# Float64 weights split on chip: two mantissa-bit steps of VectorE become a ScalarE copy and one shift-and-mask, and eight squares move to VectorE

## The chip, the cores and the metric

The kernel runs on one core of a Trainium2 chip. The metric is the device time of one execution, in microseconds; lower is better. Five engines run at the same time, each in the order of its own program: TensorE (PE, whose weight loads the profile lists as PEld), VectorE (DVE), ScalarE (ACT), GpSimd (POOL) and SyncE (SP, which here only issues transfers). They wait for each other through semaphores.

## The reference

Three layers follow each other: masked attention over 4 batches, 8 heads, 576 positions and 64 columns; a dense layer with a squared ReLU; and a mixture of 8 experts.

```
scores = scale * q @ k.T ; scores = where(mask, scores, -1e9)   # half of the heads local, half strided
attn = softmax(scores) @ v                      # -> x, 2304 tokens x 512
h = x @ w_in ; r = max(h, 0) ; g = s * (r * r) + b ; x = g @ w_out       # w_in, w_out: float64
skip_score = x @ w_skip ; e = argmax(x @ w_gate)
out = x + gate * relu(x @ w1[e]) @ w2[e]        # where skip_score > 0, else out = x
```

`w_in` (512 x 2048) and `w_out` (2048 x 512) come as 64-bit floats and are converted on the chip.

## The kernel before

**Products.** Each 32-bit matrix is kept as an upper part in the form that TensorE reads (F32R) and the rest that the upper part leaves; a product is three matmuls: upper with upper, upper with rest, rest with upper.

**Dense layer.** The 2304 tokens are 6 blocks of 384 and the 2048 hidden columns are 16 chunks. A step `i` is one block with one chunk: `mm1` (12 matmuls into tile `h`), `relu`, the square, `g_hi` and `g_lo` (upper part and rest), then `mm2` (9 matmuls that add into `x2p0` to `x2p2`). Steps 0 to 7 are block 0 with chunks 0 to 7; steps 8 to 23 are block 1 with all chunks; then block 0 goes on. So step 8 is the first that reads block 1's tokens and takes weights that step 0 has used already. After step 7 three copies (`keep`) set block 0's sums aside.

**Attention.** 32 pairs of heads, three units each. The 24 units of batches 0 and 1 come first, around steps 0 to 7. A unit is `scores` (PE, tile `sc`), `top` and `bias` (DVE), `exps` (ACT, one instruction pair per slice), `eps`, `recip`, `norm` (DVE), `turned` (PE, tile `pt`), `moved` (ACT, tile `pts`), `mixed` (PE, tile `xo`), and `put` (ACT and DVE, into `xb`, the dense layer's input). In the second batch `sc`, `pt`, `pts` and `xo` have one buffer each: the next unit's scores wait until the exponentials of the last have read theirs. Block 1's tokens are complete only when the last unit of batch 1 has been put.

**Weights.** The 32 chunks of `w_in` and `w_out` arrive as raw 64-bit words in one of three staging buffers. A word is read as a low and a high 32-bit half (`lw`, `hw`). `scale` (ACT) multiplies the high half by a power of two, which moves the exponent; `shift`, `sign` and `low` (DVE) move it three bits up, and bring in the sign and the three top bits of the low half; `upper` (ACT, or DVE for chunks 0 to 7) and `rest` (DVE) make the two parts.

**Order.** A planner (`Plan.order`) places every task by its estimated cost, its dependencies, its buffers and a priority, on the first engine that is free among those that it may run on. The programs of all engines come out of this one list. So a changed task moves the others on all engines.

Of the kernel before, what the change touches and what calls it, by code (L numbers as in the profile page):

```python
# [8 lines left out]
F32R = mybir.dt.float32r  # L9
BF16 = mybir.dt.bfloat16  # L10
I32 = mybir.dt.int32
AF = mybir.ActivationFunctionType
ALU = mybir.AluOpType
AX = mybir.AxisListType
# [13 lines left out]

PTS_N, HI_N, LO_N, NORM_N = 1, 8, 4, 0

BYPE, SQ_A = 8, 8


FIRST = (-1000.0, 0.0, 26.0, 48.0)
# [119 lines left out]
def kernel(  # L154
# [18 lines left out]
    PE, V, A, G, SY = nc.tensor, nc.vector, nc.scalar, nc.gpsimd, nc.sync  # L173
# [3 lines left out]
    x2d = dp.tile([NT, DM], F32, name="x2d")  # L177
    lst = dp.tile([NE * NT, 2], I32, name="lst")

# [20 lines left out]
    idb = ident.bitcast(BF16)[:, 1::2]  # L200
    toks = wp.tile([128, NTT], I32, name="toks")

# [3 lines left out]
    plan = Plan(CAPS)  # L206
    pools = {"s_": sp, "pts": sp, "r": sp, "sm": sp, "gh": gp, "gl": gp, "row": rp, "lo": rp, "h": ph, "sc": pm, "pt": pm, "xo": pm}

    def make(b, shape, dt):
        tag = b.tag  # L210
        pool = pools.get(tag) or (px if tag.startswith("x2p") else wp)
        return pool.tile(shape, dt, name=tag, bufs=CAPS.get(tag, 1))


    def c_pe(n, k=1, f32=True):
        return {"PE": k * ((4 if f32 else 1) * n / 2400 + 0.008)}

    def c_v(n, fast=1, psum=0.0):
        return {"V": 0.06 + n / fast / 960 + psum}

    def c_a(n, psum=False):
        return {"A": (0.13 if psum else 0.16) + n / 1400}
# [4 lines left out]
    def c_dma(n):  # L227
        return {"SP": max(0.06, n / 360e3)}
# [3 lines left out]
    def copy(e, dst, src):  # L232
        if e == "A":
            A.copy(dst, src)  # L234
        else:
            ENG[e].tensor_copy(dst, src)
# [76 lines left out]
    def add_unit(n, b, hp, g, loc, qk, vt, vbuf, qbuf, nq, nk, by_pe, prio, lq, lv):  # L313
# [40 lines left out]
        def exps(e):  # L354
# [3 lines left out]
            for i in range(nt):  # L358
                A.activation(sv[:, i, :], src[:, i, :], AF.Exp, bias=sm[0:nq, i:i + 1], scale=0.125, accum_out=sm[0:nq, 4 + i:5 + i])

# [87 lines left out]
    def fill(e):  # L448
        d_fill[0] = make(fill_b, [128, 2 * NE * NT // 128], I32)
        G.memset(d_fill[0][:], NOWHERE)  # L450
# [5 lines left out]
    t = plan.add({"G": 0.3}, fill, 6, take=[fill_b])  # L456
# [4 lines left out]

    order = [("i", 0), ("i", 1)]
    for c in range(NFC):
        order.append(("o", c))
# [3 lines left out]
    for n, (m, c) in enumerate(order):  # L470

        z = max(n, len(order) - NSTG + n % NSTG)
        raw_b, c_b = Buf([f"w{order[z][0]}{order[z][1]}"]), Buf(["row", "lo"])
        w_b = wbuf[m, c] = Buf([f"w{m}{c}"])
        wt = win_t if m == "i" else wout_t
        prio = min(PLACE[0, c], PLACE[1, c]) - LEAD + (0.5 if m == "o" else 0.0)
        d = {}

        def stage(e, d=d, raw_b=raw_b, m=m, c=c):
            raw = make(raw_b, [128, 1024], I32)  # L480
            SY.dma_start(raw[:], (w_in if m == "i" else w_out)[:, c].bitcast(I32))
            rv = raw[:].rearrange("p (n t) -> p n t", t=2)
            d["lw"], d["hw"] = rv[:, :, 0], rv[:, :, 1]

        def scale(e, d=d, c_b=c_b):
            c_ = make(c_b, [128, 512], I32)
            d["ci"], d["cv"] = c_[:], c_[:].bitcast(F32)
            A.mul(d["cv"], d["hw"].bitcast(F32), 2.0 ** -112)

        def shift(e, d=d):  # L490
            V.tensor_scalar(d["ci"], d["ci"], 3, 0x7FFFFFF8, op0=ALU.logical_shift_left, op1=ALU.bitwise_and)

        def sign(e, d=d):
            V.scalar_tensor_tensor(d["ci"], d["hw"], -(1 << 31), d["ci"], op0=ALU.bitwise_and, op1=ALU.bitwise_or)  # L494

        def low(e, d=d):
            V.scalar_tensor_tensor(d["ci"], d["lw"], 29, d["ci"], op0=ALU.logical_shift_right, op1=ALU.bitwise_or)

        def upper(e, d=d, w_b=w_b, wt=wt, c=c):
            wt[c] = make(w_b, [128, 2, 512], F32R)  # L500
            copy(e, wt[c][:, 0, :], d["cv"])

        def rest(e, d=d, wt=wt, c=c):
            ENG[e].tensor_tensor(wt[c][:, 1, :], d["cv"], wt[c][:, 0, :].bitcast(F32), op=ALU.subtract)

        t = plan.add(c_dma(128 * 8 * 512), stage, prio - 2, take=[raw_b], lat=DMA)
        t = plan.add(c_a(512), scale, prio, after=[t], take=[c_b], use=[raw_b])
        t = plan.add(c_v(512, 2), shift, prio, after=[t], use=[c_b])
        t = plan.add(c_v(512), sign, prio, after=[t], use=[c_b, raw_b])
        t = plan.add(c_v(512), low, prio, after=[t], use=[c_b, raw_b])  # L510
        t = plan.add({**c_a(512), **(c_v(512, 2) if c < HI_N else {})}, upper, prio, after=[t], take=[w_b], use=[c_b])
        w_done[m, c] = [plan.add(c_v(512), rest, prio, after=[t], use=[c_b])]

# [133 lines left out]
    def route_exp(blk):  # L647
        d = rt[blk]
        d["x8"] = sp.tile([128, 3, 8], F32, name="x8")
        A.activation(d["x8"][:], d["lg"][:, :, 0:8], AF.Exp)  # L650

# [143 lines left out]
    def up(N, f0=0, f1=NFE):  # L795
        for f in range(f0, f1):
# [6 lines left out]
            h = K["h"][f]  # L803
            A.activation(h[:, 0, 0:N], p[:, 0:N], AF.Relu)  # L804
            V.scalar_tensor_tensor(h[:, 1, 0:N], p[:, 0:N], 0.0, h[:, 0, 0:N].bitcast(F32), op0=ALU.max, op1=ALU.subtract)  # L805
# [210 lines left out]
    for i, (blk, fc, begins, ends) in enumerate(SEQ):  # L1016
        h_b, r_b, gh_b, gl_b = Buf(["h"]), Buf(["r"]), Buf(["gh"]), Buf(["gl"])
        d = {}
# [12 lines left out]
        def relu(e, d=d, r_b=r_b):  # L1031
            d["r"] = make(r_b, [128, BLK], F32)
            A.activation(d["r"][:], d["p"][:, 0:BLK], AF.Relu)  # L1033

# [3 lines left out]
        def g_hi(e, d=d, i=i, gh_b=gh_b):  # L1038
            gh = make(gh_b, [128, BLK], F32R)
            A.activation(gh[:], d["r"][:], AF.Identity, bias=sbc[:, 1:2])  # L1040
            gt[i] = [gh]
# [6 lines left out]
        def square_a(e, d=d):  # L1048
            A.activation(d["r"][:], d["r"][:], AF.Square)

# [24 lines left out]
        after = [mm1s[-1] if mm1s else None] + (x_tasks[blk] if fc == 0 else [])  # L1075
        m1 = plan.add(c_pe(BLK, 12, False), mm1, i - 3000, after=after + (w_done["i", fc] if blk < 2 else []), take=[h_b], use=[wbuf["i", fc]])
        mm1s.append(m1)
        t = plan.add(c_a(BLK, True), relu, i - 9000, after=[m1], take=[r_b], use=[h_b])
        if i < SQ_A:
            t = plan.add(c_a(BLK), square_a, i - 9000, after=[t], use=[r_b])  # L1080
            t = plan.add(c_v(BLK, 2), scale_g, i - 9000, after=[t, consts], use=[r_b])
        else:
            t = plan.add(c_v(BLK), square, i - 9000, after=[t, consts], use=[r_b])
        t = plan.add(c_a(BLK), g_hi_a if i < SQ_A else g_hi, i - 9000, after=[t], take=[gh_b], use=[r_b])
        t = plan.add(c_v(BLK), g_lo_a if i < SQ_A else g_lo, i - 9000, after=[t], take=[gl_b], use=[r_b, gh_b])
        gts[i] = t
        if i < NS - 2:
            t = plan.add(c_pe(DM, 9, False), mm2, i + 1.2 - 3000, after=[t, mm2s[-1] if mm2s else None] + (w_done["o", fc] if blk < 2 else []),
                         take=xbuf if begins else [], use=[gh_b, gl_b, wbuf["o", fc]])
# [170 lines left out]
```

## Time and profile before

| | |
|---|---|
| time before, median of 3 runs | 763.52 us (763.04 to 766.59) |
| profiled execution, its own time | 763.24 us |
| its span, first to last instruction | 761.4 us |
| TensorE busy | 734.9 us, 97% of the span |
| VectorE busy | 375.4 us, 49% |
| ScalarE busy | 296.0 us, 39% |

The busy shares are means over the whole span. The work on weights lies in the first 140 us, and what an engine lacks there is read from that stretch.

### The profile page before, as it was taken

The page shows a single profiled execution, that of the slowest core. Times are in us where ns is not written, and L with a number is a line of the kernel's source. Part 1 is how long each engine was busy: PE and PEld are TensorE (multiplying, and loading weights), DVE is VectorE, ACT ScalarE, POOL GpSimd, SP SyncE. Part 2 cuts the span into 40 slices and gives each one's busy share as a digit, 9 for nine tenths or more (in the row PEclk, how much of TensorE's full clock was granted, in tenths as well). Part 3 has the DMA queues.
Part 4 walks back from the last instruction along what each step waited for, and adds up shares of the span by engine and source line. Part 5 has one row for each costly group of instructions (what it writes and reads, how often), then busy time and mean ns, then how long its engine had stood idle before and what let it go on. Part 6 is the DMA issues. An engine that isn't in the chain of part 4 may idle for free.

```text
span 761.4 us, 11904 instructions
## 1 busy us (share of the span) xinstructions
PE 734.9 (97%) x4410; PEld 633.1 (83%) x4411; DVE 375.4 (49%) x1009; ACT 296.0 (39%) x813; POOL 62.7 (8%) x67
## 2 busy tenths in 40 slices
PE   9899989999999999999999999999999999999992
PEld 6788779998888888888888999898787888888791
DVE  4899999624565644456554324654442222313120
ACT  4787766424343543445453223533301402112020
POOL 0000000000010100010001002010032212011121
PEclk9999999999999999999999999999999999999997
DMA  9676685102231222012020005320214502011130
GB/s 294 221 208 207 201 280 142 51 0 84 76 113 48 71 65 80 27 48 78 27 84 1 2 1 174 107 80 5 79 36 142 220 37 75 14 42 56 43 72 32
DMA packets 23505, 69.00 MB, mean 91 GB/s; under 512 B 5035, under 2 KB 5291, under 8 KB 23430
## 3 DMA queue, kind: packets, MB, share of 16 engines
q1 hardware_dynamic: 19350, 56.81, 22.7%
q0 software_dynamic: 3936, 11.03, 4.7%
q8 instruction: 41, 0.67, 0.4%
q14 instruction: 34, 0.28, 0.1%
q10 hardware_dynamic: 144, 0.22, 0.1%
HBM read 52.94 MB, written 15.11 MB: 89 GB/s over the span
## 4 chain that ended last, share of the span: by engine, by line
PE 85%; DMA 5%; DVE 4%; issue 4%; ACT 1%; POOL 0%; POOLq 0%; DVEq 0%; ACTq 0%
PE h L1028 26%; PE x2p L1071 25%; PE h L801 10%; PE x2p L814 9%; DMA out<-row,ids 5%; PE sc L341 3%; PE xo L390 2%; PE pt L373 2%; PE sc L599 1%; PE pt L585 1%; PE h L1180 1%; PE h L341 1%; PE x2p L864 1%; PE h L1024 1%; DVE row L494 0%
## 5 line engine op out<-in xcount | busy, mean ns | idle before, releaser
L1028 PE MATMUL h<-xb,wi 128*128 128x384 f32 x1152 | 225.1, 344 | 2.0 <-ACT wi L234 1.2
L1028 PEld LDWEIGHTS h<-xb,wi 128*128 128x128 f32 x1152 | 203.9, 189 | 8.1 <-ACT wi L234 1.7
L1071 PE MATMUL x2p<-wo,gh 128*128 128x512 f32 x564 | 194.6, 399 | 0.0
L1071 PEld LDWEIGHTS x2p<-wo,gh 128*128 128x128 f32 x564 | 106.1, 188 | 20.1
L1071 PE MATMUL x2p<-wo,gl 128*128 128x512 f32 x282 | 111.1, 394 | 0.6 <-DVE gl L1061 0.4
L801 PE MATMUL h<-xb,wi 128*128 128x512 f32 (+1 forms) x480 | 103.3, 374 | 2.3 <-DVE row L818 1.8
L801 PEld LDWEIGHTS h<-xb,wi 128*128 128x128 f32 x480 | 83.4, 188 | 20.6 <-issue 2.8
L814 PE MATMUL x2p<-wi,wo 128*128 128x512 f32 x432 | 99.4, 390 | 0.0
L1036 DVE SCALAR_TENSOR_TENSOR r<-r,sbc 128x384 f32<-128x384 f32 x88 | 54.3, 617 | 85.7 <-ACT r L1033 85.6
L814 PEld LDWEIGHTS x2p<-wi,wo 128*128 128x128 f32 x432 | 80.8, 188 | 16.6
L1033 ACT ACTIVATE r<-h 128x384 f32<-128x384 f32 x96 | 47.0, 489 | 116.5 <-PE h L1028 111.2
L1040 ACT ACTIVATE gh<-r,sbc 128x384 fp32r<-128x384 f32 x88 | 54.3, 617 | 77.5 <-PE x2p L1071 53.6
L1045 DVE SCALAR_TENSOR_TENSOR gl<-r,sbc,gh 128x384 fp32r<-128x384 f32 x88 | 54.3, 617 | 59.1 <-ACT gh L1040 57.8
L804 ACT ACTIVATE wo<-h 128x512 fp32r<-128x512 f32 (+1 forms) x40 | 22.2, 554 | 144.0 <-PE h L801 139.1
L805 DVE SCALAR_TENSOR_TENSOR wo<-h,wo 128x512 fp32r<-128x512 f32 (+1 forms) x40 | 25.5, 638 | 76.5 <-ACT wo L804 72.3
L1071 PEld LDWEIGHTS x2p<-wo,gl 128*128 128x128 f32 x282 | 53.1, 188 | 9.4 <-DVE gl L1061 0.7
L703 POOL DMA_INDIRECT lst<-pay,ii x18 | 18.4, 1020 | 466.1 <-DVE ii L697 444.9
L818 DVE SCALAR_TENSOR_TENSOR row<-x2p,ids,xb 128x512 f32<-128x512 f32 x14 | 10.5, 751 | 61.8 <-PE x2p L814 61.8
L390 PEld LDWEIGHTS xo<-pts,vl 96*64 96x64 f32 (+1 forms) x480 | 16.9, 135 | 12.5 <-issue 4.5
L390 PE MATMUL xo<-pts,vl 96*64 96x64 f32 (+1 forms) x480 | 21.6, 226 | 3.6 <-DVE xb L397 2.1
L819 POOL DMA_INDIRECT out<-row,ids x14 | 13.9, 995 | 107.5 <-DVE row L818 93.2
L397 DVE TENSOR_TENSOR xb<-xo,xb 128x192 fp32r<-128x192 f32 (+4 forms) x59 | 18.3, 336 | 5.8 <-ACT xb L234 5.6
(479 smaller groups left out, 769.1 us busy)
## 6 DMA issues: line engine op xcount, KB each, us to landing
wo<-in_w SPq DMA_DIRECT2D x16, 512.0 KB, 5.8
qks<-in_qkstr SPq DMA_DIRECT2D x7, 882.0 KB, 6.5
wo<-in_w_out SPq DMA_DIRECT2D x12, 512.0 KB, 3.7
x2d<-row SPq DMA_DIRECT2D x21, 256.0 KB, 3.9
qkl<-in_qkloc SPq DMA_DIRECT2D x6, 864.0 KB
wo<-in_w_in SPq DMA_DIRECT2D x10, 512.0 KB, 4.0
out<-row SPq DMA_DIRECT2D x18, 256.0 KB, 2.0
wi<-in_w_in SPq DMA_DIRECT2D x6, 512.0 KB
```

What stands on the lines that cost most here:

```text
L341: PE.matmul(sc[0:nq, i * nk:(i + 1) * nk], qt, qk[0][:, k0:k0 + nk], start=not by_pe, stop=not by_pe or i == nt - 1)
L390: PE.matmul(xo[64 * h:64 * h + 64, c:c + m], vt[h][:, t, :], d["pts"][0:nk, r:r + m], start=True, stop=True)
L801: PE.matmul(p[:, 0:N], W[f][:, w, k * 128:(k + 1) * 128], x[:, k, 0:N], start=n == 0, stop=n == 11)
L804: A.activation(h[:, 0, 0:N], p[:, 0:N], AF.Relu)
L805: V.scalar_tensor_tensor(h[:, 1, 0:N], p[:, 0:N], 0.0, h[:, 0, 0:N].bitcast(F32), op0=ALU.max, op1=ALU.subtract)
L814: PE.matmul(y[:], K["h"][f][:, g, c], W[NFE + f][:, w, :], start=n == 0, stop=n == 3 * NFE - 1)
L1028: PE.matmul(p[:, 0:BLK], win_t[fc][:, w, k * 128:(k + 1) * 128], x[:, k, :], start=n == 0, stop=n == 11)
L1033: A.activation(d["r"][:], d["p"][:, 0:BLK], AF.Relu)
L1036: V.scalar_tensor_tensor(d["r"][:], d["r"][:], sbc[:, 0:1], d["r"][:], op0=ALU.mult, op1=ALU.mult)
L1040: A.activation(gh[:], d["r"][:], AF.Identity, bias=sbc[:, 1:2])
L1045: V.scalar_tensor_tensor(gl[:], d["r"][:], sbc[:, 1:2], gt[i][0][:].bitcast(F32), op0=ALU.add, op1=ALU.subtract)
L1071: PE.matmul(x2p[t][:], g[:, c], wout_t[fc][:, w, :], start=begins and n == 0, stop=ends and n == 2)
```

## The change

The first four chunks that are converted keep the old steps. For the other 28, after `scale` has read the high half, ScalarE copies the upper 16 bits of the low half over the lower 16 bits of the high half (`beside`); VectorE then shifts the high half right by 13 with its sign kept and masks it, so that the sign and the three bits stand where they belong (`ends`, in place in the staging buffer, every second 32-bit word); and `merge` shifts the scaled value and joins it. Before, three VectorE instructions stood there (`shift`, `sign`, `low`), now two of VectorE and one of ScalarE.

`SQ_A` goes from 8 to 0: steps 0 to 7 no longer square on ScalarE (`square_a`, then `scale_g` on VectorE, a plain copy `g_hi_a` and a subtraction `g_lo_a`), but as the later steps do (`square` on VectorE, `g_hi` with a bias on ScalarE, `g_lo` on VectorE).

```diff
-BYPE, SQ_A = 8, 8
+BYPE, SQ_A = 8, 0
+
+ODD = 4
...
+            hv = raw[:].bitcast(U16).rearrange("p (n t) -> p n t", t=4)
+            d["from"], d["to"] = hv[:, :, 1], hv[:, :, 2]
...
+        def beside(e, d=d):
+            A.copy(d["to"], d["from"])
+
+        def ends(e, d=d):
+            V.tensor_scalar(d["hw"], d["hw"], 13, 7 - (1 << 31), op0=ALU.arith_shift_right, op1=ALU.bitwise_and)
+
+        def merge(e, d=d):
+            V.scalar_tensor_tensor(d["ci"], d["ci"], 3, d["hw"], op0=ALU.logical_shift_left, op1=ALU.bitwise_or)
...
-        t = plan.add(c_v(512, 2), shift, prio, after=[t], use=[c_b])
-        t = plan.add(c_v(512), sign, prio, after=[t], use=[c_b, raw_b])
-        t = plan.add(c_v(512), low, prio, after=[t], use=[c_b, raw_b])
+        if n < ODD:
+            t = plan.add(c_v(512, 2), shift, prio, after=[t], use=[c_b])
+            t = plan.add(c_v(512), sign, prio, after=[t], use=[c_b, raw_b])
+            t = plan.add(c_v(512), low, prio, after=[t], use=[c_b, raw_b])
+        else:
+            t = plan.add(c_a(512), beside, prio, after=[t], use=[raw_b])
+            t = plan.add(c_v(512, 2), ends, prio, after=[t], use=[raw_b])
+            t = plan.add(c_v(512), merge, prio, after=[t], use=[c_b, raw_b])
```

All engines' programs are the same up to step 0 (about 40 us in the trace), and TensorE's program is the same again from step 8 on. Between them it holds the same matmuls in another order. In the rows below, line numbers of the changed kernel are 3 higher in the attention part and 22 higher in the dense part.

ScalarE, between the exponentials of the last unit but one and those of the last unit of batch 1. Before there are four instructions between them: the last copy `g_hi_a` of step 7, a `scale`, an `upper` and the `pts` copy of an earlier unit.

```order
L359 ACTIVATE s__1369,sm<-sc,sm 108x54 x4
L1056 CAST gh<-r 128x384
L488 ACTIVATE row<-wi_1336 128x512
L234 CAST wo_1396<-row 128x512
L234 COPY pts<-pt 54x432
L359 ACTIVATE s__1424,sm<-sc,sm 108x54 x3
```

In the changed kernel there are ten at that place (L508 is `beside`, L237 a copy: into `row` one of the three `keep` copies, into `wo` and `wi` three `upper`, into `xb` two of `put`, into `pts` two `moved`).

```order
L362 ACTIVATE s__1399,sm<-sc,sm 108x54 x4
L508 COPY wo_1352<-wo_1352 128x512
L237 COPY row<-x2p_843 128x512
L237 COPY pts<-pt 54x432
L237 CAST wo_1429<-lo 128x512
L237 CAST wi_1443<-row 128x512
L237 CAST wo_1453<-row 128x512
L237 CAST xb_89<-xo 128x12x6
L237 CAST xb_90<-xo 128x12x12
L237 COPY pts<-pt 54x432
L237 COPY row<-x2p_847 128x512
L362 ACTIVATE s__1470,sm<-sc,sm 108x54 x3
```

Ahead of the first of these rows the changed program has, from the `relu` of step 7 on, eight more: `relu`, the exponentials of the unit before, `scale`, `g_hi`, `beside`, `scale`, `beside`, `scale`. Behind the last row it has, up to the last unit's `pts` copy: two `scale`, one `xb` copy, two `beside`, and the `pts` copy.

TensorE, the end of batch 1's attention. Before, `mm2` of step 6 (chunk 6, nine matmuls, not shown) stands ahead of the last unit's scores, and `mm2` of step 7 (`wo_1396`, nine matmuls of which the first is shown) between the last units' transposes.

```order
L341 MATMUL sc<-qks 108x54 x3
L373 MATMUL pt<-im,s__1313 54x108 x4
L390 MATMUL xo<-pts,vl 64x54 x8
L373 MATMUL pt<-im,s__1369 54x108 x4
L1071 MATMUL x2p_871<-wo_1396,gh 128x512
```

In the changed kernel `mm2` of step 6 stands ahead of `mm1` of step 7, and `mm2` of step 7 (the first row here is its last matmul) ahead of the last unit's scores; what is left between them and step 8 is attention alone. The last row is `mm1` of step 8.

```order
L1093 MATMUL x2p_851<-wo_1328,gh 128x512
L376 MATMUL pt<-im,s__1355 54x108 x4
L339 LDWEIGHTS im
L339 MATMUL sc<-im 108x162
L344 MATMUL sc<-qks 108x54 x3
L393 MATMUL xo<-pts,vl 64x54 x8
L376 MATMUL pt<-im,s__1399 54x108 x4
L393 MATMUL xo<-pts,vl 64x54 x8
L376 MATMUL pt<-im,s__1470 54x108 x3
L393 MATMUL xo<-pts,vl 64x54 x4
L393 MATMUL xo<-pts,vl 64x36 x2
L1050 MATMUL h<-xb_89,wi_644 128x384 x12
```

So one `mm2` of the dense layer moved from behind step 7's `mm1` to ahead of it, and none is left between the last units' attention steps.

## Rows read from the trace of the kernel before

**Rows 1.** The page: busy time of engines; one group of instructions.

```profile
PE 734.9 (97%) x4410; PEld 633.1 (83%) x4411; DVE 375.4 (49%) x1009; ACT 296.0 (39%) x813; POOL 62.7 (8%) x67
...
L1036 DVE SCALAR_TENSOR_TENSOR r<-r,sbc 128x384 f32<-128x384 f32 x88 | 54.3, 617 | 85.7 <-ACT r L1033 85.6
```

**Rows 2.** Stretches: length, busy PE PEld DVE ACT POOL (count), clock, DMA, GB/s.

```profile
37.30:40.70 3.40, 3.40 (x12) 3.34 (x13) 3.40 (x11) 1.60 (x7) 0.00 (x0) 0.55 0.80 257
40.70:90.00 49.30, 48.32 (x384) 40.48 (x382) 46.36 (x123) 38.30 (x122) 0.00 (x0) 1.00 0.66 210
90.00:103.20 13.20, 8.92 (x90) 7.01 (x89) 12.70 (x36) 10.30 (x33) 0.00 (x0) 1.00 0.77 266
103.20:153.00 49.80, 49.58 (x252) 45.26 (x252) 41.64 (x77) 28.38 (x52) 0.00 (x0) 1.00 0.42 127
```

**Rows 3.** What PE waited for from 37.3 to 103.2 us: total, times, longest.

```profile
PE xo L390 <- DVE xb L397: 2.1, 1, 2.1
PE pt L373 <- DVE sm L352: 0.8, 1, 0.8
```

**Rows 4.** Timeline of PE: start, length, what, count, [idle before]; step 7 to step 8.

```profile
37.29 3.40 PE L1028 MATMUL h<-xb,wi 128*128 128x384 f32 x10 [0.80 <-DVE wi L504]
...
86.90 2.47 PE L1028 MATMUL h<-xb,wi 128*128 128x384 f32 x12
89.31 0.57 PE L390 MATMUL xo<-pts,vl 96*64 96x64 f32 x12
...
90.64 0.48 PE L1071 MATMUL x2p<-wo,gh 128*128 128x512 f32 x1
...
93.66 0.23 PE L336 MATMUL sc<-im 108*108 108x162 bf16 x1 [0.70 <-ACT s__1369 L359]
...
102.68 0.54 PE L390 MATMUL xo<-pts,vl 54*64 54x54 f32 x12 [2.08 <-DVE xb L397]
103.15 6.62 PE L1028 MATMUL h<-xb,wi 128*128 128x384 f32 x36
```

**Rows 5.** ACT's groups from 37.3 to 140 us: busy, mean ns.

```profile
L488 ACT ACTIVATE row<-wo 128x512 f32<-128x512 f32 x15 | 10.2, 681 | 1.3 <-DMA wo<-in_w_in 0.8 <-DMA wo<-in_w_out 0.5
...
L1040 ACT ACTIVATE gh<-r,sbc 128x384 fp32r<-128x384 f32 x9 | 5.5, 613 | 5.6 <-DVE r L1036 5.0 <-PE h L1028 0.5
L1049 ACT ACTIVATE r<-r 128x384 f32<-128x384 f32 x8 | 4.3, 534 | 0.0
L1056 ACT CAST gh<-r 128x384 fp32r<-128x384 f32 x8 | 4.1, 516 | 0.0
```

**Rows 6.** DVE's groups from 37.3 to 103.2 us: busy, mean ns.

```profile
L494 DVE SCALAR_TENSOR_TENSOR row<-wo,row 128x512 int32<-128x512 int32 x9 | 6.2, 689 | 0.0
...
L491 DVE TENSOR_SCALAR row<-row 128x512 int32<-128x512 int32 x13 | 5.5, 423 | 0.1
L1061 DVE TENSOR_TENSOR gl<-r,gh 128x384 fp32r<-128x384 f32 x8 | 4.4, 554 | 0.0
...
L1052 DVE TENSOR_SCALAR r<-r,sbc 128x384 f32<-128x384 f32 x8 | 3.8, 473 | 0.3 <-ACT r L1049 0.3
```

**Rows 7.** Timeline of ACT, step 7's relu to the last unit's pts copy.

```profile
90.14 0.62 ACT L234 CAST wi<-lo 128x512 fp32r<-128x512 f32 x1
90.66 0.49 ACT L1033 ACTIVATE r<-h 128x384 f32<-128x384 f32 x1
91.04 0.67 ACT L488 ACTIVATE row<-wo 128x512 f32<-128x512 f32 x1
91.60 0.52 ACT L1049 ACTIVATE r<-r 128x384 f32<-128x384 f32 x1
92.35 0.31 ACT L359 ACTIVATE s__1369<-sc,sm 108x54 f32<-108x54 f32 x1 [0.22 <-DVE sm L352]
...
93.49 0.52 ACT L1056 CAST gh<-r 128x384 fp32r<-128x384 f32 x1
...
101.72 0.47 ACT L234 COPY pts<-pt 54x324 f32<-54x324 f32 x1
```

More of the change, by code (lines that the diff above doesn't have):

```diff
@@ L11 @@
 I32 = mybir.dt.int32
+U16 = mybir.dt.uint16
 AF = mybir.ActivationFunctionType
```

## Prediction

> **What bounds the kernel now.** I read the busy shares first: TensorE is busy 97% of the span [rows 1], so a change can win only where TensorE stands idle, and can lose wherever it makes TensorE stand. Then the busy time by stretch. From 103.2 us on TensorE is full: 49.58 of 49.80 us [rows 2]. The work on weights goes on there, with VectorE busy 41.64 of 49.80 us, but nobody waits for it. Before 103.2 us it is not full: 49.30 less 48.32 is 0.98 us of idle from 40.7 to 90 us, and 13.20 less 8.92 is 4.28 us from 90 to 103.2 us, while VectorE is busy 46.36 of 49.30 and 12.70 of 13.20 us and ScalarE 38.30 and 10.30 us [rows 2]. So VectorE is the engine that is short there, and ScalarE has the room. Third, the waits: the longest are for VectorE, 2.1 us for a `put` that frees `xo`, and 0.8 us for a norm [rows 3].
>
> After that comes the order. TensorE's program is the same from step 8 on, and full there, so what the change is worth is by how much step 8 starts earlier or later than 103.15 us [rows 4].
>
> **The change part by part: busy time.** Of each of 28 chunks VectorE loses three instructions (423 + 689 + 689 ns) and gets two. `merge` has the form of `sign`: 689 ns. `ends` has the form of `shift`, with every second word in place of a contiguous tile: 423 ns if that makes no difference, 689 ns if it runs at the rate of `sign`, which also reads every second word [rows 6]. I take 423, the row of the same operation with one source and a constant. The Trainium skill (VectorE: DVE Perf Modes, section Mode 2×_2P) says that an operation with one tensor source in SBUF can take two 32-bit elements at a time, and names an even outer dimension as a condition, not a step of one; the contiguous 423 ns beside 689 ns agrees, and no run so far shows the strided case. So VectorE is relieved of 0.69 us a chunk, or of 0.42 us at the other bound. One instruction starts about 0.09 us before the last one's mean duration is over, so the relief in time is nearer to 0.60 us.
>
> ScalarE gets one `beside` a chunk. No row shows a 16-bit copy with a step in its output. The nearest is `scale`, same 512 elements, read with the same step: 681 ns, next start after 0.56 us [rows 5, 7]; the contiguous cast is 620 ns, next start after 0.52 us [rows 7]. I take 0.56, with 0.45 (a relu of 384 columns takes 0.38) and 0.70 as bounds. The Trainium skill (ScalarE: Activation LUTs, section What ACT_TABLE_LOAD costs) gives 186 ns and 0.833 ns an element for an ACTIVATE with constant scale: 612 ns by estimate, where the row with a strided read has 681; the measurement decides, and by the page each copy would cost 0.07 us less, the piece summed below 0.35 us less.
>
> Squares: in steps 0 to 7 VectorE's 473 + 554 ns become 617 + 617 [rows 1, 6], 0.21 us more a step (the later steps' `g_lo` is taken as long as their `square`, the same operation); ScalarE's 534 + 516 become 613 [rows 5], 0.44 us less. Over all, VectorE gets about 28 x 0.60 - 8 x 0.21 = 15 us lighter, ScalarE 28 x 0.56 - 8 x 0.44 = 12 us heavier. On busy time alone this looks like a gain of up to the 5.3 us of idle.
>
> **On the path: the end of the attention.** Nothing moves ahead of 40.7 us, where TensorE also runs at the low one of its clock levels (granted 0.55 from 37.3 to 40.7 us, ten matmuls in 3.40 us [rows 2, 4]). What moves is the place of the last units. I measure from the end of step 7's `mm1`, 89.31 us, to step 8's start, 103.15 us: 13.84 us, of which 4.28 us idle and about 9.55 us work [rows 2, 4]. That work holds `mm2` of step 6, from 90.64 us to 92.96 us (0.70 us of wait ahead of 93.66), 2.32 us [rows 4]. In the changed program this `mm2` stands ahead of step 7's `mm1`, and the rest of the set is the same. So, with no other difference, step 7's `mm1` ends at 89.31 + 2.32 = 91.63 us, and 7.23 us of TensorE's work are left until step 8.
>
> But ScalarE's queue is longer there. From step 7's `relu`, which can't start before `mm1` ends, to the last unit's `pts` copy, for which the last `mixed` and then step 8 wait, ScalarE's changed program has 26 instructions. By their start-to-start times: `relu` 0.38; exponentials 4 + 4 + 3 slices, 1.14 us for four (92.35 to 93.49), so 3.14; five `scale` at 0.56, 2.80; five `beside` at 0.56, 2.80; `g_hi` 0.613 less the overlap of 0.09, 0.52; three `upper` at 0.52, 1.56; two `keep` copies as long as those, 1.04; two `pts` copies of 432 columns, between the 0.38 of 384 and the 0.52 of 512 columns, 0.86; `xb` copies 0.55 (by length); the last `pts` copy in full, 0.47 [rows 5, 7]. Sum 14.12 us. With two handovers of 0.05 to 0.10 us and the last `mixed` of 0.47 us (102.68 to 103.15 [rows 4]) step 8 can't start earlier than 14.7 us after step 7's `mm1`. Before, ScalarE needed 102.19 - 90.66 = 11.53 us for the same piece, waits included [rows 7].
>
> Following the three queues through it by hand, with the same durations, I find ScalarE the last one at nearly every handover: five fillers (`scale` and `beside` of later chunks) stand ahead of the exponentials of the last unit but one, and ten instructions between those and the last unit's. These fillers belong to chunks 8 to 11, which nobody needs for 30 us; they stand in order all the same. VectorE's queue has gaps there.
>
> Step 8 then starts at 91.63 + 14.7 = 106.3 us, 3.2 us later than before. Two small terms I let cancel: the 0.98 us of idle from 40.7 to 90 us may fall away by half or so, since VectorE is lighter; and a ScalarE that has some 10 us more to do there adds waits of its own, estimated at half a microsecond. After step 8 nothing differs: two chunks' work per two steps has room on both engines, since the weights of steps 8 to 15 are ready, and more chunks are done by then than before. So the profiled execution of 763.24 us would become 766.4, and the median of 763.52 us, which is 0.28 above it, **766.8 us**.
>
> **The rivals.** *The idle goes away.* VectorE is what the waits name; if the lighter queue serves each norm, top and put at once, all 0.98 + 4.28 us of idle vanish: 758.3 us. For it speaks that VectorE is busy 96% from 90 to 103.2 us [rows 2]; against it the sum of ScalarE's queue. It decides only where that piece takes less than 13.84 - 2.32 = 11.5 us: with all five copies at nothing the sum is still 14.7 - 2.8 = 11.9 us. So it needs ScalarE's other instructions to be shorter too, or step 7's `mm1` to end earlier by more than I see.
>
> *The loss is smaller.* Copies at 0.45 us (0.55 off the piece), the whole 0.98 us regained and no new waits: 3.2 - 0.55 - 0.98 = 1.7 us later, 765.2 us.
>
> *The clock falls.* In the piece TensorE has 7.2 us of work in 14.7 us. Before step 0 it stood 0.80 us and more, with little between, and ran at 1.2 GHz up to 40.7 us; ten matmuls took 3.40 us where twelve take 2.47 at 2.4 GHz [rows 2, 4], a loss of 3.40 - 2.06 = 1.3 us. The idle of 2.08 us at 102.68 did not bring this on: 36 matmuls in 6.62 us behind it [rows 4]. With more idle it may: 768.1 us.
>
> *The new steps are dearer.* `ends` at 0.60 us start to start brings VectorE's queue in the piece (43 instructions, about 13 us by the same kind of sum) to 14.3 us with five of them in it, as long as ScalarE's; `beside` at 0.70 adds 0.7 us to ScalarE's; a `scale` that waits for its transfer, as ScalarE does in places now (1.3 us in all for 15 of them [rows 5]), blocks the exponentials behind it. Together 1 to 3 us more: 768.8 us. By this one the change would not relieve VectorE as it says.
>
> **Chances and range.** About half a per cent, 3.8 us, is what a measurement of this kernel tells from no change. The forecast, 765.5 to 768.3 us: 0.42. Smaller loss: 0.15. Idle gone: 0.11. Clock: 0.14. Dearer steps: 0.18. Slower by over 0.5% (above 767.3): the last two and a quarter of the first, 0.42. Faster by over 0.5%: 0.11. Within: 0.47. The range from 761.5 to 770.5 us leaves out most of the faster case and the far end of the dearer steps, about 2 in 10; the forecast's own is 765.5 to 768.3.
>
> **What the changed profile would show.** Right: VectorE's busy share falls well under nine tenths from 40 to 100 us and ScalarE's rises; step 8 starts near 106 us with TensorE idle 7 us or more in the 15 us before; the waits ahead of the last units name ScalarE (`pts`, the exponentials); `beside` near 680 ns, `ends` near 420. Wrong: step 8 at or before 103 us, or step 7's `mm1` ending well before 91 us; a second stretch of low clock at step 8 would be the clock rival; `ends` near 690 ns the dearer one. The forecast fails most easily if ScalarE's copies are much shorter than `scale`, or if TensorE loses or wins time between 40 and 90 us that I took as even.

## The result, and the profile after

| | before | changed |
|---|---|---|
| median | 763.46 us (4 runs, 763.04 to 766.59) | 773.53 us (4 runs, 771.89 to 774.02) |
| ratio | | 1.0119, interval 1.0088 to 1.015 |
| profiled execution, span | 763.24, 761.4 us | 771.89, 770.1 us |

Slower by 1.2%, and outside the stated range (761.5 to 770.5 us). The ratio is taken over all runs, so it is not the quotient of the medians. The profiled execution lost 8.65 us, of which 3.2 were forecast.

The page of the changed kernel: busy times, shares of the chain that ended last, and the group of the new copy `beside`.

```profile
PE 741.0 (96%) x4410; PEld 637.3 (83%) x4411; DVE 364.2 (47%) x982; ACT 321.7 (42%) x832; POOL 62.8 (8%) x67
...
PE 78%; ACT 8%; DMA 7%; issue 4%; DVE 2%; SPq 0%; POOL 0%; POOLq 0%; ACTq 0%; DVEq 0%
...
L508 ACT COPY wo<-wo 128x512 uint16<-128x512 uint16 x20 | 27.9, 1395 | 0.1
```

Against [rows 1], VectorE is 11.2 us lighter (15 were forecast) and ScalarE 25.7 us heavier (12 were forecast). The copy takes 1395 ns, about twice the 681 of `scale`, which had stood for it. It stands twice in the groups (20 and 8 times, by its tile). In the chain ScalarE's share is 8%; in the kernel before it was 1%:

```profile
PE 85%; DMA 5%; DVE 4%; issue 4%; ACT 1%; POOL 0%; POOLq 0%; DVEq 0%; ACTq 0%
```

Stretches of the changed kernel; columns as in [rows 2].

```profile
40.70:90.00 49.30, 48.37 (x367) 39.75 (x364) 42.37 (x109) 48.83 (x121) 0.00 (x0) 1.00 0.67 210
90.00:103.20 13.20, 9.59 (x64) 7.28 (x62) 10.94 (x30) 13.08 (x36) 0.00 (x0) 0.74 0.77 242
103.20:153.00 49.80, 45.90 (x238) 41.56 (x239) 32.87 (x64) 37.20 (x64) 0.00 (x0) 0.90 0.42 131
95.00:100.00 5.00, 5.00 (x19) 4.03 (x18) 2.94 (x9) 4.97 (x14) 0.00 (x0) 0.50 0.53 139
105.00:110.00 5.00, 2.58 (x18) 2.13 (x19) 3.31 (x9) 4.11 (x9) 0.00 (x0) 0.50 0.72 260
110.00:115.00 5.00, 5.00 (x20) 5.00 (x20) 3.62 (x8) 3.89 (x6) 0.00 (x0) 0.63 0.93 281
```

ScalarE is now the full engine (48.83 of 49.30 and 13.08 of 13.20 us) and VectorE has room (42.37 and 10.94 us): the change moved the limit from one engine to the other. From 103.2 us on TensorE is no longer full, and in three of these pieces its granted clock is 0.50 to 0.63; before, it was 1.00 in the same stretches [rows 2].

What TensorE waited for in the changed kernel from 30 to 150 us, the three longest.

```profile
PE xo L393 <- ACT pts L237: 2.2, 2, 2.0
PE xo L393 <- DVE xb L400: 2.1, 1, 2.1
PE sc L339 <- ACT s__1355 L362: 1.7, 1, 1.7
```

Two of the three name ScalarE. Before, the longest one named VectorE [rows 3].

TensorE's timeline in the changed kernel, from step 7's `mm1` (first row) to step 11's (last row):

```profile
87.94 2.46 PE L1050 MATMUL h<-xb,wi 128*128 128x384 f32 x12
...
92.61 0.25 PE L339 MATMUL sc<-im 108*108 108x216 bf16 x1 [1.72 <-ACT s__1355 L362]
...
103.67 1.10 PE L393 MATMUL xo<-pts,vl 54*64 54x54 f32 x16 [2.13 <-DVE xb L400]
...
108.14 0.86 PE L393 MATMUL xo<-pts,vl 54*64 54x54 f32 x12 [2.00 <-ACT pts L237]
108.93 8.77 PE L1050 MATMUL h<-xb,wi 128*128 128x384 f32 x36
118.32 0.49 PE L1093 MATMUL x2p<-wo,gh 128*128 128x512 f32 x1 [0.63 <-ACT gh L1062]
...
120.94 2.28 PE L1050 MATMUL h<-xb,wi 128*128 128x384 f32 x12
```

The row that answers to the last one in the kernel before, by the same view:

```profile
112.18 2.28 PE L1028 MATMUL h<-xb,wi 128*128 128x384 f32 x12
```

So up to step 11's `mm1` the changed kernel has lost 120.94 - 112.18 = 8.76 us, and its span is 770.1 - 761.4 = 8.7 us longer: the loss is complete there. It divides at the rows of [rows 4] into four parts:

| | before | changed | difference |
|---|---|---|---|
| step 7's `mm1` ends | 89.31 | 87.94 + 2.46 = 90.40 | +1.09 |
| from there to step 8 | 13.84 | 108.93 - 90.40 = 18.53 | +4.69 |
| `mm1` of steps 8 to 10, 36 matmuls | 6.62 | 8.77 | +2.15 |
| from their end to step 11's `mm1` | 2.41 | 3.24 | +0.83 |

The 89.31 is the start of the row behind `mm1`; by that measure the changed kernel has 90.33, and 0.07 us go from the first part to the second.

ScalarE's timeline in the second part, from step 7's `relu` to the last unit's `pts` copy (L508 is `beside`, L496 `scale`):

```profile
90.93 0.48 ACT L1055 ACTIVATE r<-h 128x384 f32<-128x384 f32 x1
...
93.50 1.38 ACT L508 COPY wo<-wo 128x512 uint16<-128x512 uint16 x1
94.57 0.76 ACT L496 ACTIVATE lo<-wi 128x512 f32<-128x512 f32 x1
95.36 1.37 ACT L508 COPY wi<-wi 128x512 uint16<-128x512 uint16 x1
...
98.18 1.39 ACT L508 COPY wo<-wo 128x512 uint16<-128x512 uint16 x1
99.24 0.76 ACT L237 COPY row<-x2p 128x512 f32<-128x512 f32 x1
...
106.42 1.46 ACT L508 COPY wi<-wi 128x512 uint16<-128x512 uint16 x1
107.56 0.53 ACT L237 COPY pts<-pt 54x324 f32<-54x324 f32 x1
```

There is no idle in it: 107.56 + 0.53 - 90.93 = 17.16 us. One `beside` holds the next instruction up by 1.06 to 1.14 us (93.50 to 94.57, 95.36 to 96.45), although its own 1.38 us reach further. The last two stand right ahead of the `pts` copy for which TensorE waits 2.00 us.

VectorE's groups of `merge` (L514) and `ends` (L511) from 37 to 150 us:

```profile
L514 DVE SCALAR_TENSOR_TENSOR row<-row,wo 128x512 int32<-128x512 int32 x15 | 10.3, 687 | 0.1
L511 DVE TENSOR_SCALAR wo<-wo 128x512 int32<-128x512 int32 x20 | 8.6, 428 | 10.6 <-ACT wo L508 10.5
```

These two cost what was taken, 689 and 423 ns. The Trainium skill (VectorE: DVE Perf Modes, section Mode 2×_2P) asks nothing of the step, and the strided `ends` at 428 ns agrees; its 10.6 us of idle behind `beside` show VectorE waiting for the copy.

### The profile page after: what moved, and what is told of

It reads as the page before. It is cut to its first block, busy times and chain, and to the rows that moved or that the text cites. A ratio compares the mean times of both kernels' runs of the same rounds, so it can differ in the third digit from the quotient of the medians.

```text
span 770.1 us, 11899 instructions
## 1 busy us (share of the span) xinstructions
PE 741.0 (96%) x4410; PEld 637.3 (83%) x4411; DVE 364.2 (47%) x982; ACT 321.7 (42%) x832; POOL 62.8 (8%) x67
## 4 chain that ended last, share of the span: by engine, by line
PE 78%; ACT 8%; DMA 7%; issue 4%; DVE 2%; SPq 0%; POOL 0%; POOLq 0%; ACTq 0%; DVEq 0%
PE h L1050 24%; PE x2p L1093 23%; PE h L823 10%; PE x2p L836 8%; DMA out<-row,ids 5%; PE sc L344 3%; ACT wo L508 2%; PE xo L393 2%; PE pt L376 1%; DMA qks<-in_qkstr 1%; ACT row L496 1%; PE sc L621 1%; PE pt L607 1%; DMA wi<-in_w_out 1%; ACT wi L508 1%
## 5 line engine op out<-in xcount | busy, mean ns | idle before, releaser
L1058 DVE SCALAR_TENSOR_TENSOR r<-r,sbc 128x384 f32<-128x384 f32 x96 | 59.2, 616 | 89.6 <-ACT r L1055 89.3
L1062 ACT ACTIVATE gh<-r,sbc 128x384 fp32r<-128x384 f32 x96 | 59.6, 620 | 74.2 <-PE x2p L1093 54.3
L1067 DVE SCALAR_TENSOR_TENSOR gl<-r,sbc,gh 128x384 fp32r<-128x384 f32 x96 | 59.2, 616 | 61.9 <-ACT gh L1062 60.7
L725 POOL DMA_INDIRECT lst<-pay,ii x18 | 18.5, 1026 | 474.8 <-DVE ii L719 453.5
L508 ACT COPY wo<-wo 128x512 uint16<-128x512 uint16 x20 | 27.9, 1395 | 0.1
```

The costliest lines, as they stand in the source:

```text
L508: A.copy(d["to"], d["from"])
L1058: V.scalar_tensor_tensor(d["r"][:], d["r"][:], sbc[:, 0:1], d["r"][:], op0=ALU.mult, op1=ALU.mult)
L1067: V.scalar_tensor_tensor(gl[:], d["r"][:], sbc[:, 1:2], gt[i][0][:].bitcast(F32), op0=ALU.add, op1=ALU.subtract)
```

## The experiments

Four theories stand against each other. *Length* (the expectations' theory 1): the copies are long, and delay what is queued behind them on ScalarE. *Order* (theory O): not the work but the changed order costs. *Fillers*: whatever the engine, conversions of chunks that nobody needs yet stand in the queues ahead of the last units' steps, and the loss goes when they are held back. *Clock*: the loss at step 8 is the granted clock's; no run tests this one by itself, it is read from the rows. Ratios are against runs of the kernel before on the same chip, in three series whose medians of it were 765.28, 765.67 and 764.34 us; an edit is shown against the changed kernel, or against the one before where it says so.

### What makes the copy long

Each form of the copy, alone, three times ahead of the kernel's work, which runs behind it in full.

```diff
...
+        for _ in range(3):
+            A.copy(q4(0, 2), q4(0, 1))
+            A.copy(q4(0, 2, 256), q4(0, 1, 256))
+            A.copy(q4(1, 2), q4(0, 1))
+            A.copy(c1(1), q4(0, 1))
+            A.copy(q4(1, 2), c1(0))
+            A.copy(c1(1), c1(0))
+            A.copy(q2(1, 1), q2(0, 0))
+            A.copy(w32(0, 1), w32(0, 0))
+            A.copy(w32(1, 1), w32(0, 0))
+            A.copy(b4(0, 2), b4(0, 1))
+            V.tensor_copy(q4(2, 2), q4(2, 1))
+            G.tensor_copy(q4(2, 2), q4(2, 1))
```

The first number of a call is the tile (2 is tile 0 again). `q4` is every fourth 16-bit half (a step of 8 bytes), `q2` every second one (4 bytes), `c1` contiguous halves, `w32` every second 32-bit word (8 bytes), `b4` as `q4` in bf16. The lines L1213 to L1224 follow this order.

> The changed kernel with copies on scratch data put ahead of all work, three of each, every shape on a line of its own: the beside copy (512 16-bit elements, read and written at a step of 8 bytes, in place), the same with 256 elements, the same into another tile, strided read into a contiguous output, contiguous read into a strided output, contiguous to contiguous, a step of 4 bytes, 32-bit words at a step of 8 bytes in place and into another tile, bf16 in place of uint16, and the same 16-bit copy on VectorE and on GpSimd. It does the kernel's work too; its total time says nothing. In the changed kernel the copy takes 1395 ns, where I took 681. Theory A, the strided 16-bit output costs: the forms with a strided 16-bit output take about 1400 ns whatever is read, the others 600 to 700 ns, and the 32-bit form 680 ns. Theory B, the strided 16-bit read costs: the contiguous output takes 1400 ns too and the contiguous read 600. Theory C, the number type costs: all uint16 forms take 1400 ns and bf16 680. Theory D, reading and writing the same words costs: the form into another tile falls to 700 ns.

ScalarE's groups in the first 60 us; the fourth number of a row is the mean in ns.

```profile
L1215 ACT COPY qks<-qkl 128x512 uint16<-128x512 uint16 x3 | 4.2, 1413 | 0.0
L1213 ACT COPY qkl<-qkl 128x512 uint16<-128x512 uint16 x3 | 4.1, 1352 | 4.7 <-POOL qkl L1224 4.4 <-DVE qkl L1203 0.3
L1222 ACT COPY qkl<-qkl 128x512 bf16<-128x512 bf16 x3 | 4.0, 1334 | 0.0
L1217 ACT COPY qks<-qkl 128x512 uint16<-128x512 uint16 x3 | 4.0, 1326 | 0.1
...
L1214 ACT COPY qkl<-qkl 128x256 uint16<-128x256 uint16 x3 | 2.3, 763 | 0.1
L1219 ACT COPY qks<-qkl 128x512 uint16<-128x512 uint16 x3 | 2.3, 761 | 0.1
...
L1220 ACT COPY qkl<-qkl 128x512 f32<-128x512 f32 x3 | 1.9, 645 | 0.1
L1216 ACT COPY qks<-qkl 128x512 uint16<-128x512 uint16 x3 | 1.9, 644 | 0.1
L1221 ACT COPY qks<-qkl 128x512 f32<-128x512 f32 x3 | 1.9, 643 | 0.0
L1218 ACT COPY qks<-qkl 128x512 uint16<-128x512 uint16 x3 | 1.9, 618 | 0.1
```

The kernel's own form takes 1352 ns outside of all crowding (L1213), and 1413 into another tile (L1215): it is neither contention nor the overlap of source and target. With contiguous output a strided read takes 644 (L1216), hardly more than contiguous to contiguous, 618 (L1218). With strided output a contiguous read takes 1326 (L1217). Words of 32 bits at the same 8-byte step take 645 (L1220). So what costs is **16-bit output with a step**, and by the step: 761 ns at 4 bytes (L1219), 1352 at 8. bf16 behaves as uint16 (L1222). Theory A of the expectation holds. The same copy took 735 ns on VectorE and 1316 on GpSimd. The Trainium skill (ScalarE: Activation LUTs, section What ACT_TABLE_LOAD costs) gives 186 + 512 × 0.833 = 612 ns for an ACTIVATE with constant scale, an estimate from its figures: the contiguous row's 618 agrees, the 1326 to 1413 of stepped 16-bit output do not.

### The same order with short copies

The copy takes 176 of 512 elements (the other 336 are left out), to come near what the prediction had assumed; the programs are otherwise the same.

```diff
-            A.copy(d["to"], d["from"])
+            A.copy(d["to"][:, 0:176], d["from"][:, 0:176])
```

> The changed kernel with the same order of all instructions, but each beside copies 176 of its 512 elements, so that it should take about 0.5 to 0.6 us start to start, near the 0.56 us that the prediction took; the converted weights are wrong in their last bits. Theory 1, the length of the copy is what the prediction missed: step 8 starts near 106 us and the time is 765 to 768 us, close to the 766.8 predicted. Rival theory 2, the new order itself holds the units up whatever the copy costs: the time stays above 771 us.

767.73 us (10 runs, 766.52 to 768.54), ratio 1.0039, interval 1.0023 to 1.0055. ScalarE's group of it, and rows of its timeline:

```profile
L508 ACT COPY wo<-wo 128x176 uint16<-128x176 uint16 x20 | 11.8, 590 | 0.1
```

```profile
92.64 0.60 ACT L508 COPY wo<-wo 128x176 uint16<-128x176 uint16 x1
92.96 0.72 ACT L496 ACTIVATE lo<-wi 128x512 f32<-128x512 f32 x1
...
102.31 0.66 ACT L496 ACTIVATE row<-wi 128x512 f32<-128x512 f32 x1 [0.87 <-DMA x2d<-row]
```

Step 7's `mm1` ended at 90.04 us and step 8 began at 105.16, 15.12 us later; the prediction had 14.7 for copies of 0.56 us from start to start. That the two are near each other is in part chance. These copies hold the queue for 0.31 to 0.40 us each (92.64 to 92.96), 1.71 us for the five where 2.80 had been summed, so the prediction's sum would give 13.6 here. What comes on top is 0.87 us in which a `scale` waits for a transfer that frees its tile, 0.35 of other instructions and 0.32 of the last `mixed` at the low clock. The clock fell here too (36 matmuls in 8.66 us). So of the 1.19% that the change cost, 0.80 are the length of the copies (1.0119 against 1.0039), about 6 us (771.89 - 767.16 = 4.73 us between the two profiled executions). In the piece up to step 8 the five copies differ by 5.45 - 1.71 = 3.74 us, and 2.65 of these are beyond what the prediction had for them.

### One part alone

Squares on VectorE only (`ODD = 32`), or the new weight steps only (`SQ_A = 8`), in the order that the planner gives.

```diff
-ODD = 4
+ODD = 32
```

> Only the squares' part of the change: all 32 chunks converted by shift, sign and low as before, steps 0 to 7 squared on VectorE. Theory 1: VectorE gets 8 x 0.21 us, ScalarE loses 3.5 us; within 2 us of before, 762 to 766 us. Rival theory 3, the squares on VectorE bring the loss: 768 us or more.

```diff
-BYPE, SQ_A = 8, 0
+BYPE, SQ_A = 8, 8
```

> Only the weights' part of the change: beside, ends and merge for 28 chunks, steps 0 to 7 squared on ScalarE as before. Theory 1: ScalarE has 3.5 us more to do than in the changed kernel, and it is the full engine, so the time is as long or longer, 772 to 777 us. Rival theory 3: 763 to 767 us.

The squares alone cost as much as the whole change: 772.79 us (4 runs), ratio 1.0106, interval 1.0071 to 1.0142. That was a miss; 0.21 us a step had been counted for them. The weights alone: 773.79 us, 1.0124, 1.0088 to 1.016, as theory 1 had it, with one wait of 4.0 us for a norm and step 8 at 110.97 us. The parts don't add up (1.06 and 1.24% alone, 1.19 together): each brings an order of its own, and no run shows why.

VectorE's timeline in the squares' kernel, at the last unit but one. Its `eps` (first L365 row), `recip` (first L368 row) and `norm` (L371) should follow each other; its exponentials ended on ScalarE at 100.48 us.

```profile
100.67 0.68 DVE L239 COPY row<-x2p 128x512 f32<-128x512 f32 x1
101.28 0.16 DVE L365 TENSOR_SCALAR sm<-sm 108x4 f32<-108x4 f32 x1
101.34 0.42 DVE L499 TENSOR_SCALAR lo<-lo 128x512 int32<-128x512 int32 x1
101.68 0.57 DVE L400 TENSOR_TENSOR xb<-xo,xb 128x72 fp32r<-128x72 f32 x2
102.17 0.17 DVE L368 RECIPROCAL sm<-sm 108x4 f32<-108x4 f32 x1
102.25 0.29 DVE L352 TENSOR_REDUCE sm<-sc 108x3 f32<-108x162 f32 x1
102.47 0.68 DVE L502 SCALAR_TENSOR_TENSOR lo<-wo,lo 128x512 int32<-128x512 int32 x1
103.06 0.37 DVE L371 TENSOR_TENSOR s__1413<-s__1413,sm 108x216 f32<-108x216 f32 x1
```

`norm` ends at 103.43 us, 2.95 us after the exponentials; the three instructions that the unit needs are 0.16 + 0.17 + 0.37 us long. Between them stand a copy of 0.68 (`keep`), a `shift`, two `put`, a `top` and a `sign`. TensorE waited 2.27 us at that place; the profile puts the wait down to `bias`, the instruction right behind `norm`.

### The work in the old order

The kernel before, program for program, with the instructions' work exchanged in place. Squares (ScalarE's place of `square_a` stays empty), against the kernel before:

```diff
-            A.activation(d["r"][:], d["r"][:], AF.Square)
+            pass
...
-            V.tensor_scalar(d["r"][:], d["r"][:], sbc[:, 0:1], sbc[:, 1:2], op0=ALU.mult, op1=ALU.add)
+            square(e, d)
...
-            A.copy(gh[:], d["r"][:])
+            A.activation(gh[:], d["r"][:], AF.Identity, bias=sbc[:, 1:2])
...
-            V.tensor_tensor(gl[:], d["r"][:], gt[i][0][:].bitcast(F32), op=ALU.subtract)
+            V.scalar_tensor_tensor(gl[:], d["r"][:], sbc[:, 1:2], gt[i][0][:].bitcast(F32), op0=ALU.add, op1=ALU.subtract)
```

> The squares' part of the change alone, but in the order of the kernel before on every engine: steps 0 to 7 squared on VectorE and ScalarE's square left out of its place. Squares alone with the order that the planner makes of them took 772.8 us. Theory O, the order that the planner makes of the squares' part is what costs there, since the added work is 0.21 us of VectorE a step: 762 to 766 us. Rival theory S, the work on VectorE itself costs: 769 us or more.

764.18 us (10 runs, 763.72 to 768.09), ratio 0.9995, interval 0.9977 to 1.0013: nothing. What the squares cost alone is the order they bring.

Weights, against the kernel before: `beside` directly behind each `scale`, `ends` in the place of `shift`, `merge` in that of `low`.

```diff
         def scale(e, d=d, c_b=c_b, new=n >= 4):
...
+            if new:
+                A.copy(d["to"], d["from"])
...
         def shift(e, d=d, new=n >= 4):
+            if new:
+                V.tensor_scalar(d["hw"], d["hw"], 13, 7 - (1 << 31), op0=ALU.arith_shift_right, op1=ALU.bitwise_and)
+                return
...
         def sign(e, d=d, new=n >= 4):
+            if new:
+                return
...
         def low(e, d=d, new=n >= 4):
+            if new:
+                V.scalar_tensor_tensor(d["ci"], d["ci"], 3, d["hw"], op0=ALU.logical_shift_left, op1=ALU.bitwise_or)
+                return
```

> The weights' part of the change alone, in the order of the kernel before: beside right behind each scale, ends in the place of shift, nothing in the place of sign, merge in the place of low. Theory 1, the 1.3 us copies overload ScalarE whatever the order: some 19 of them fall before step 8, 25 us more on an engine that is busy 50 of 66 us there, so 770 us or more. Rival theory O, the order is what costs in this part too: 762 to 766 us.

777.12 us (4 runs), ratio 1.0162, interval 1.0136 to 1.0187: the worst of all. Here it is the work. With the copy cut to 176 elements as above:

> The weights' part in the order of the kernel before, but each beside copies 176 of 512 elements (0.5 to 0.6 us); the converted weights are wrong in their last bits. With whole copies this took 777 us. Theory 1, the copy's length is all of that loss: 760 to 766 us, and if VectorE's relief is worth something with a cheap copy, below 763. Rival, the third step on ScalarE costs by its place right behind each scale: 769 us or more.

767.64 us (6 runs), ratio 1.0038, interval 1.0019 to 1.0056, a little above what was expected. The 36 matmuls took 6.62 us, but step 8 began at 108.47, with 2.9 us of waits for `pts` copies. So a copy of 590 ns, which holds ScalarE's queue for some 0.33 us, doesn't pay either in this place, though VectorE is relieved.

### Holding the fillers back

Conversions of chunks 8 to 15 may not begin before the last `mixed` of batch 1; the programs follow from that.

```diff
-        t = plan.add(c_a(512), scale, prio, after=[t], take=[c_b], use=[raw_b])
+        t = plan.add(c_a(512), scale, prio, after=[t] + (o_tasks[7][-1:] if c >= 8 else []), take=[c_b], use=[raw_b])
```

> The changed kernel, but the conversions of chunks 8 to 15 may start only after the last mixed of batch 1, so none of their scale, beside and upper stands ahead of the last units on ScalarE; TensorE's tasks and all other work are the same. Theory 1 with the fillers: ScalarE's queue from step 7's relu to the last pts copy falls by some 10 us, step 8 starts near 100 to 103 us, and the time is 759 to 765 us. Rival theory 2, the chain of the last units itself takes that long, with or without fillers: 769 us or more.

764.89 us (10 runs), ratio 1.0004, interval 0.9989 to 1.0019: no slower than the kernel before, with copies of 1409 ns and all 28 chunks in the new form. Two stretches of it, and its step 8:

```profile
90.00:103.20 13.20, 9.60 (x102) 7.87 (x101) 6.26 (x23) 7.83 (x34) 0.00 (x0) 0.94 0.52 184
105.00:110.00 5.00, 5.00 (x21) 5.00 (x20) 3.26 (x7) 4.97 (x7) 0.00 (x0) 0.64 0.24 53
```

```profile
102.84 9.18 PE L1050 MATMUL h<-xb,wi 128*128 128x384 f32 x36
```

ScalarE's 13.08 us from 90 to 103.2 have become 7.83, and step 8 starts at 102.84 us. The clock fell behind it all the same (0.64; 36 matmuls in 9.18 us).

The same edit in the squares' kernel:

> The squares' part alone in the planner's own order (772.8 us), with the conversions of chunks 8 to 15 held back until after the last mixed of batch 1. If that order loses by fillers ahead of the last units, here on VectorE: 760 to 766 us. If it loses by the chain of the last units alone: 770 us or more.

765.96 us (10 runs), ratio 1.0022, interval 1.0009 to 1.0034, against 1.0106 without. In the lines above it was VectorE's queue that held fillers; the hold-back takes them from every engine, so this run doesn't tell the engines apart.

And in the kernel before:

> The kernel before, with one thing changed: the conversions of chunks 8 to 15 may start only after the last mixed of batch 1. Theory 1 with the fillers: the kernel before has fillers on VectorE ahead of its last units too, so step 8 starts 1 to 4 us earlier and the time falls to 759 to 763 us. Rival: their place costs nothing before, because VectorE must do them anyway, and the later conversions hold up steps 16 on: 764 us or more.

759.80 us (6 runs, 759.51 to 760.97), ratio **0.9944**, interval 0.9926 to 0.9961: better than both kernels. TensorE in it, a stretch (columns as in [rows 2]) and the timeline at step 8:

```profile
90.00:103.20 13.20, 11.79 (x105) 10.16 (x105) 10.31 (x32) 9.08 (x30) 0.00 (x0) 1.00 0.68 226
```

```profile
99.26 0.54 PE L390 MATMUL xo<-pts,vl 54*64 54x54 f32 x12 [0.94 <-DVE xb L397]
99.73 6.62 PE L1028 MATMUL h<-xb,wi 128*128 128x384 f32 x36
...
108.77 2.28 PE L1028 MATMUL h<-xb,wi 128*128 128x384 f32 x12
```

Of the 4.28 us of idle that the kernel before has in this stretch [rows 2], 1.41 are left. Step 8 begins 3.42 us earlier than in [rows 4], the span (757.9 us) is 3.5 us shorter, and the wait of 2.08 us for a `put` has become 0.94. All six runs had a mean granted clock of 0.989 or more. The four runs of the kernel before in the same series with 0.990 or more took 763.00 to 763.96 us, so about 3.4 us of the gain are not the clock's.

This kernel is also the one that the two held-back ones have to be compared with. The same dependency gains 0.56% in the kernel before, so with it everywhere the whole change still loses 0.6% (1.0004 against 0.9944) and the squares alone 0.8% (1.0022 against 0.9944). By these ratios the fillers are about half of the change's loss, and a smaller part of the squares'. What is left has not been tested. In the traces, the held-back changed kernel begins step 8 3.11 us later (102.84 against 99.73) and takes 2.56 us more for the 36 matmuls. From the end of step 7's `mm1` to step 8 the two need nearly the same, 11.37 and 10.78 us, but the changed one stands idle for 3.60 us of it and the other for 1.41: `mm2` of step 6, which could fill the waits, is done ahead of `mm1` there.

### Telling the planner the price

`beside` was planned as any ScalarE instruction of 512 columns. With its measured price:

```diff
-            t = plan.add(c_a(512), beside, prio, after=[t], use=[raw_b])
+            t = plan.add({"A": 1.3}, beside, prio, after=[t], use=[raw_b])
```

> The changed kernel with the planner told what the beside copy costs, 1.3 us in place of 0.53; same work, other order. Theory 1, ScalarE is short of time whatever the order: 766 to 773 us. Rival theory O, the wrong estimate and the order that comes of it is the loss: 760 to 765 us.

771.01 us (4 runs), ratio 1.0089, interval 1.0065 to 1.0114: still a loss, and its interval overlaps that of the change itself (1.0088 to 1.015); one wait of 4.8 us for exponentials takes the place of the others. With the hold-back as well:

> The changed kernel with both: conversions of chunks 8 to 15 held back, and the planner told 1.3 us for the copy. If the fillers are the main loss and the estimate a smaller one: 758 to 764 us, below the held-back version with the wrong estimate (764.9). If ScalarE's work before step 8 is still too much: 764 to 768 us.

768.53 us (6 runs), ratio 1.006, interval 1.0039 to 1.008: worse than the hold-back without it, against expectation. There are two new waits, 2.7 us for an `upper` and 2.4 us for a norm. A truer cost is not a better order here; I did not find out why the planner chose this one.

## Why the prediction was wrong, by its steps

**The step that failed: `beside` at 0.56 us, with 0.45 and 0.70 as bounds.** It was the operation without a row, taken from `scale`, which *reads* with a step. It *writes* 16 bits with a step, and that was no detail: 1395 ns, 1.06 to 1.14 us from start to start, outside both bounds. The five in the piece from step 7's `relu` to the last `pts` copy come to 5.45 us where 2.80 had been summed.

**The sum of that piece: right in its other terms.** 17.16 us against 14.12; `beside` makes 2.65 of the difference, all the other instructions 0.39. ScalarE was without idle in it, so the queue was the path, as forecast. Around it, `relu` began 0.53 us after `mm1`'s end, behind a cast still running (at most 0.10 had been allowed), and the last `mixed` took 0.79 in place of 0.47 us at the low clock. So the mechanism was right and this term of the sum mis-sized. The kernel with short copies bears out the direction, not the number: that its ratio, 1.0039, comes near the forecast (766.8 / 763.52 = 1.0043) is luck, since its copies were cheaper than the 0.56, a transfer cost 0.87 us, `mm1` ended 1.59 us earlier than forecast and the low clock took 2.04 us on the 36 matmuls.

**Step 7's `mm1` at 91.63 us** ended at 90.40, 1.23 us earlier: step 0 began at 36.44 us instead of 37.29, and its ten matmuls took 3.01 us instead of 3.40. Nothing was to move ahead of 40.7 us. That it is the change that moved it is not shown: the programs up to there are the same, the held-back changed kernel began these matmuls at 37.23 us, and all traces but the probe's lie between 36.18 and 37.77. From step 0's end to `mm1`'s the time was as forecast.

**VectorE relieved, `ends` at 423, `merge` at 689 ns:** right (428 and 687), and worth nothing here, since ScalarE took over as the full engine. The 12 us that ScalarE was to gain became 25.7.

**Squares at 0.21 us a step:** right as work (ratio 0.9995 in the old order), wrong as an edit: in the planner's order they cost 1.06% alone. Only the order of both edits together had gone into the sum, so this didn't harm it.

**The clock rival (chance 0.14, +1.3 us)** came true on top of the forecast: granted 0.50 to 0.63 around step 8, 2.15 us on 36 matmuls. I had priced it as another case, not as something that may come with the longer idle that I forecast myself. A sign was wrong with it: TensorE was to stand idle 7 us or more in the 15 before step 8. It stood 6.7 us in the 18.5, since its work there took 11.8 us at the lower clock in place of 7.2; this delayed nothing but the last `mixed`, because ScalarE's queue was longer. *Dearer steps* named `beside` up to 0.70 from start to start, where it is 1.06 to 1.14.

**The idle goes away** stayed out, but the hold-back in the kernel before shows that 2.87 of the 4.28 us could be had with the same work, by starting conversions later.

The miss in the profiled execution, 771.89 - 766.4 = 5.5 us: -1.23 (`mm1` earlier), +3.83 (18.53 against 14.7), +2.15 (the clock), +0.83 (behind step 10). "After step 8 nothing differs" held from step 11 on.

What stays open: that stepped 16-bit output is slow was measured, not explained; what the change still loses with the fillers held back was not tested; and what brings the clock down was only observed. In the held-back changed kernel it fell with TensorE busy 9.60 of 13.20 us, in the kernel before, at 8.92 of 13.20 us, it did not.

## What to carry to other kernels

Look at the *output* of an instruction without a row: element size and step, not its length alone; if no row has that form, the bounds have to reach to a multiple, and a probe of one instruction settles it. When work moves to the engine that "has room", sum the queue of that engine between the two waits that matter; a busy share over the stretch doesn't show which instructions stand ahead of the chain. Where engines run in order, ask first which work in front of a latency chain isn't needed yet: one dependency that held it back gained 0.56% here, where the edits to the work lost. And try such a remedy on the kernel before too: against that, the change had still not paid.

## What the runs showed of the hardware

ScalarE's stepped 16-bit output: 761 ns at 4 bytes and 1326 to 1413 at 8, where 512 elements otherwise take 618 to 645. In the changed kernel an instruction behind such a copy starts about 0.3 us before the copy's recorded end (1.38 long, 1.07 to the next start), where it is 0.09 us otherwise; so in that queue it costs less than its row says. In the probe, where the next copy writes the same tile, the next start came 0.04 us behind the end (1.35 long, 1.39 to the next start).

The granted clock differs between executions of one and the same kernel. Of the 51 runs of the kernel before in the three series, the 13 with a mean clock of 0.990 or more took 762.37 to 765.87 us (median 763.04), and the 11 at 0.980 or 0.981 took 765.95 to 767.25 (median 766.6). The one whose profile I had read was at 0.990. The profile of the squares in the old order is of an execution at 0.980, its longest (768.09 us), and shows a stretch at the low level: granted 0.76, 0.50, 0.50 and 0.88 in the four 5-us stretches from 95 to 115 us, and 36 matmuls in 8.77 us. By these figures the kernel before, too, pays some 3 to 4 us for such a stretch in some executions; no trace of it shows one. All four runs of the changed kernel were at 0.979 or 0.980, so a part of its loss may be that it pays in every one of them.
